# Packed attention and a gated MLP: the first attention re-tiled, its softmax in 32x32 blocks, and its queues in another order

## The chip, the core and the metric

The kernel runs on one core of a Trainium2 chip. The metric is the device time of one execution in microseconds (us). The engines are PE (TensorE, matmuls into PSUM), DVE (VectorE), ACT (ScalarE), POOL (GpSimd) and SP (which here only issues transfers). Each engine works off its own queue in order. An instruction that waits holds up all that stands behind it on its engine.

## The reference

Eight batches of eight heads are attended twice: 32 packed queries p attend to 576 keys and values, and the 576 queries then attend to the 32 results. A gated MLP follows over all 4608 rows.

```python
p_packed = sm_attn(p, k, v)            # per batch and head: 32 x 64
out = sm_attn(q, p_packed, p_packed)   # 576 x 64
x = out.transpose(0, 2, 1, 3).reshape(4608, 512)
h = x @ w_in                           # 512 -> 2048
g = h * clip(h + 3, 0, 6) / 6
return g @ w_out                       # 2048 -> 512
```

w_in and w_out arrive as 64-bit floats; the kernel makes 32-bit ones of them on the chip.

## The kernel before

**Folding.** The product of the second attention with w_in is folded: m = p_packed @ w_in is formed per batch (32 rows per head, two groups g of four heads, so 128 rows per group), and the first product of the MLP is a.T @ m, with a the second softmax. Values are split in two parts (hi, lo) so that three fast matmuls make one exact product: a_hi and a_lo, m_hi and m_lo, g_hi and g_lo (gh, gl), wo_hi and wo_lo.

**Stages.** Batch 0 goes through `first_attention` (line 456), which I call the head: transposes on PE, the packed scores `s1` (line 560), `pack` (line 612), the second scores and softmax `s2` (line 627), and the first product of step 0 by `gemm1` (line 441). `first_moe` (line 894) then runs the sixteen steps f of batch 0 (f is a block of 128 of the 2048 columns); batch 1's attention is woven in from step 4 on. The loop from line 991 does batches 1 to 7, each with the next batch's attention woven in.

**A step of `first_moe`.** PE: first product of step f (`gemm1`, twelve matmuls into the one tile ps_h0), then `u_m0` of step f+1 (line 187, needs w_in of that step), then the second products of step f-1 (`gemm2`, line 904, needs gh, gl, wo_hi, wo_lo). ACT: the Relu of line 951 reads ps_h0. DVE: the gate of line 952 reads it too and so sets it free. ACT writes gh (line 960), POOL subtracts to gl (line 962), and both do the same for the last 64 rows (bnd_hi, bnd_lo).

**Making weights.** `narrowed` (line 125) turns 64-bit words into floats in four steps: two ACT passes (lines 139 and 141), a shift on DVE (line 145), an addition on POOL (line 149). `w_in_step` does it for w_in of a step; `w_out_step` does it for w_out (tile x_out) and then writes wo_hi on ACT (line 159) and wo_lo on DVE (line 161). I write w_in(2), x_out(0), wo_hi(0) for the ones of a step. Each tile of 64-bit words has two buffers, so the load of a step waits for POOL's addition two steps back.

**What sets the order.** In the head and in steps 0 to 3 PE, DVE, ACT and POOL run in the order in which the program is written (`tc.manual_schedule`). Pieces are generators, and `step(part, n)` or `next(part)` runs one to the next `yield`, so the list of such calls (lines 724 to 799) is the order of the queues. From step 4 (IN_ORDER) on a scheduler orders the woven attention. `warm(n)` issues n matmuls of zeros; WARM holds their counts.

## Time and profile before

| | before |
|---|---|
| median of 3 runs | 757.79 us (756.15 to 761.76) |
| profiled execution | 757.65 us, span 755.9 us |
| granted clock of TensorE, mean | 0.995 |
| PE busy | 735.9 us (97%) |
| ACT busy | 387.2 us (51%) |
| DVE busy | 345.5 us (46%) |
| POOL busy | 279.9 us (37%) |
| DMA | 55.98 MB, mean 74 GB/s |

The span is the time from the first to the last instruction of the profiled execution. A busy PE is not PE at its peak, since matmuls are pipelined and their ends are modelled. The chain of work that ended last spends 79% of the span on PE, 6% on DMA and 5% on DVE. The edit lies in the first 40 us and in the first steps of `first_moe`.

### The profile page before, as it was taken

To read this page: it belongs to the slowest core of one execution; us is meant where nothing else is said; L and a number is where in the kernel's file an instruction comes from. 1 tells how busy PE (TensorE), PEld (TensorE's weight loads), DVE (VectorE), ACT (ScalarE), POOL (GpSimd) and SP (SyncE) were. 2 spreads that over 40 slices of the span, in tenths; PEclk is the share of its full clock that TensorE was granted. 3 is DMA by queue.
4 is the path that set the end of the run, shared out by engine and by line. 5 is a ranking of instruction groups with operands and counts; after the bars stand their busy time and mean duration, and the time that the engine had idled before them with its cause. 6 is when DMAs were issued, how large, how long until landed. Compare 5 with 4: busy or idle time off the path is not lost.

```text
span 755.9 us, 13998 instructions
## 1 busy us (share of the span) xinstructions
PE 735.9 (97%) x5197; PEld 581.3 (77%) x5197; DVE 345.5 (46%) x714; ACT 387.2 (51%) x922; POOL 279.9 (37%) x415
## 2 busy tenths in 40 slices
PE   7898999999999999999999999999999999999998
PEld 5775776778777876878777886788787887788886
DVE  3676888432563365342733446342643527321121
ACT  4687874543445445553455535563354635553343
POOL 0487782422233224332333223333232333343332
PEclk9999899999999999999999999999999999999999
DMA  8869964104410541043310523024220210000010
GB/s 260 254 146 215 263 186 83 56 16 93 96 32 31 102 73 45 1 91 69 63 43 1 120 52 78 1 60 96 47 61 1 61 33 29 1 29 0 2 42 29
DMA packets 191205, 55.98 MB, mean 74 GB/s; under 512 B 173216, under 2 KB 184480, under 8 KB 191136
## 3 DMA queue, kind: packets, MB, share of 16 engines
q1 hardware_dynamic: 191136, 55.08, 31.5%
q8 instruction: 41, 0.67, 0.4%
q14 instruction: 28, 0.23, 0.1%
HBM read 45.61 MB, written 9.44 MB: 73 GB/s over the span
## 4 chain that ended last, share of the span: by engine, by line
PE 79%; DMA 6%; DVE 5%; SPq 4%; ACT 3%; issue 2%; POOL 1%; DVEq 0%; POOLq 0%; ACTq 0%
PE acc L853 46%; PE ps_hh L824 23%; PE ps L265 6%; SPq L213 3%; DMA raw_in<-in_moe_w_in_dram 2%; DMA nat<-in_q_dram 2%; PE ps L320 1%; DVE tr L398 1%; DMA nat<-in_k_dram 1%; PE ps_h L448 1%; PE ps L304 1%; DMA v_nat<-in_v_dram 1%; POOL x_out L149 1%; DVE w_in_sb L145 0%; ACT raw_in L139 0%
## 5 line engine op out<-in xcount | busy, mean ns | idle before, releaser
L842 POOL TENSOR_TENSOR g<-t,g 128x256 fp32r<-128x256 f32 x224 | 168.1, 754 | 410.0 <-ACT g L841 384.5
L853 PE MATMUL acc<-wo_hi,g 128*128 128x512 f32 x896 | 316.5, 394 | 1.3 <-ACT g L841 1.3
L837 DVE SCALAR_TENSOR_TENSOR t<-t,ps_hh 128x320 f32<-128x320 f32 (+1 forms) x224 | 100.1, 449 | 252.1 <-ACT t L836 252.0
L836 ACT ACTIVATE t<-ps_hh,three 128x320 f32<-128x320 f32 (+1 forms) x224 | 112.5, 503 | 177.9 <-PE ps_hh L824 167.1
L853 PEld LDWEIGHTS acc<-wo_hi,g 128*128 128x128 f32 x896 | 167.8, 188 | 35.8 <-issue 4.0
L853 PE MATMUL acc<-wo_lo,g 128*128 128x512 f32 x448 | 177.5, 396 | 0.0
L841 ACT CAST g<-t 128x256 fp32r<-128x256 f32 x224 | 90.4, 405 | 94.1 <-DVE t L837 92.8
L824 PE MATMUL ps_hh<-a_hi,m_hi 128*128 128x320 f32 (+1 forms) x448 | 136.1, 304 | 0.5 <-DVE t L837 0.5
L824 PE MATMUL ps_hh<-a_lo,m_hi 128*128 128x320 f32 (+1 forms) x448 | 132.7, 296 | 0.0
L824 PE MATMUL ps_hh<-a_hi,m_lo 128*128 128x320 f32 (+1 forms) x448 | 132.7, 296 | 0.0
L824 PEld LDWEIGHTS ps_hh<-a_hi,m_hi 128*128 128x128 f32 x448 | 84.4, 188 | 34.5 <-issue 19.5
L853 PEld LDWEIGHTS acc<-wo_lo,g 128*128 128x128 f32 x448 | 84.5, 189 | 11.9 <-issue 1.7
L824 PEld LDWEIGHTS ps_hh<-a_lo,m_hi 128*128 128x128 f32 x448 | 84.5, 189 | 8.2 <-issue 0.9
L824 PEld LDWEIGHTS ps_hh<-a_hi,m_lo 128*128 128x128 f32 x448 | 84.5, 189 | 1.7 <-issue 1.3
L398 DVE STREAM_TRANSPOSE tr<-nat 128x576 f32<-128x576 f32 x56 | 41.9, 765 | 30.9 <-PE ps L265 13.3
L388 DVE TENSOR_TENSOR m_lo<-ps,m_hi 128x512 fp32r<-128x512 f32 x56 | 36.1, 683 | 34.8 <-ACT m_hi L387 34.8
L848 POOL TENSOR_TENSOR bnd_lo<-t,bnd_hi 128x64 fp32r<-128x64 f32 x112 | 39.3, 351 | 0.0
L387 ACT CAST m_hi<-ps 128x512 fp32r<-128x512 f32 x56 | 30.1, 589 | 9.8 <-PE ps_hh L824 7.7
L265 PE MATMUL ps<-w_in_sb,pps 64*32 64x512 f32 x448 | 34.3, 601 | 0.5 <-DVE m_lo L388 0.5
L962 POOL TENSOR_TENSOR gl<-t,gh 128x512 fp32r<-128x512 f32 x16 | 23.4, 1464 | 20.6 <-ACT gh L960 11.8
L853 PE MATMUL acc<-wo_hi,gh 128*128 128x512 f32 x64 | 27.0, 421 | 3.5 <-ACT gh L960 3.5
L149 POOL TENSOR_TENSOR w_in_sb<-w_in_sb,raw_in 128x512 int32<-128x512 int32 x14 | 19.5, 1392 | 26.6 <-ACT raw_in L141 17.7
(170 smaller groups left out, 860.2 us busy)
## 6 DMA issues: line engine op xcount, KB each, us to landing
out_dram<-osb SPq DMA_DIRECT2D x36, 256.0 KB, 2.1
nat<-in_k_dram SPq DMA_DIRECT2D x112, 72.0 KB, 2.5
nat<-in_q_dram SPq DMA_DIRECT2D x112, 72.0 KB, 2.6
raw_in<-in_moe_w_in_dram SPq DMA_DIRECT2D x14, 512.0 KB, 5.9
raw_out<-in_moe_w_out_dram SPq DMA_DIRECT2D x14, 512.0 KB, 5.4
v_nat<-in_v_dram SPq DMA_DIRECT2D x56, 128.0 KB, 2.8
spare<-in_k_dram SPq DMA_DIRECT2D x2, 512.0 KB, 4.8
raw<-in_moe_w_in_dram SPq DMA_DIRECT2D x2, 512.0 KB, 4.1
```

The costliest lines, as they stand in the source:

```text
L149: nc.gpsimd.tensor_tensor(out=xi, in0=xi, in1=low, op=ALU.add)
L265: nc.tensor.matmul(banks[x][NPK * a:NPK * a + NPK, :n], rows[half, a], c, start=True, stop=True)
L387: nc.scalar.copy(out=hi[:, x], in_=ps)
L388: nc.vector.tensor_sub(out=lo[:, x], in0=ps, in1=hi[:, x].bitcast(F32))
L398: nc.vector.transpose(out=t, in_=state.pop(("nat", which, b, a)))
L824: nc.tensor.matmul(h[:, :n], mm[:, g, fs], aa[:, t0:t0 + n], start=(g == 0 and i == 0), stop=(g == NG - 1 and i == 2),)
L836: nc.scalar.activation(out=t[:, :n], in_=h, func=AF.Relu, bias=three)
L837: nc.vector.scalar_tensor_tensor(out=t[:, :n], in0=t[:, :n], scalar=6.0, in1=h, op0=ALU.min, op1=ALU.mult)
L841: nc.scalar.copy(out=gh, in_=tm)
L842: nc.gpsimd.tensor_sub(out=gl, in0=tm, in1=gh.bitcast(F32))
L848: nc.gpsimd.tensor_sub(out=bnd_lo[:, slot:slot + REM], in0=tb, in1=bh.bitcast(F32))
L853: nc.tensor.matmul(acc, gg, ww[:, f], start=(f == 0 and i == 0), stop=(f == NF - 1 and i == 2),)
```

## The change

- Keys and queries of batch 0 are transposed two heads to a matmul (`turn_rows`, 4 matmuls of 128 rows), where the queries took 8 matmuls in halves of the array.
- Scores (`products`) and second scores have the packed rows as 32 output partitions per head; the second scores come out as 128 packed rows by 576 queries, not as queries by packed rows. The second softmax `s2` then works as in later batches: DVE transposes blocks of 32x32, takes maximum, difference and sum, and transposes back. PE's transposes of z go away. Group 0 is done in one piece (its multiplication and a_lo on POOL), group 1 in two halves (on DVE).
- `pack` computes 32 output rows per head (20 matmuls of 64 columns, where there were 10 of 128), writes the result twice beside each other, transposes once, and POOL builds the block-diagonal pp_bd and p_bd (`blocks_of`), which DVE and ACT did.
- The scores of heads 0 to 3 run before the keys of heads 4 to 7 are transposed.
- Loads: fewer and larger ones; p and the last 64 keys are issued from ACT; w_in(0) is loaded behind the last queries, not ahead of them.
- Weights: the head ends with w_in(0), w_in(1) made and only the ACT passes of x_out(0) and x_out(1) done. The rest of x_out(0) comes in step 0 ahead of gh; all of w_in(2), the rest of x_out(1) and x_out(2) come behind gh of step 0.
- The copies of t to gh and bnd_hi in a step take both halves of the rows at once, in another row order; the stores of batch 0 follow it.

```diff
-WARM = (3, 2, 2, 1, 3)
+WARM = (3, 2, 3, 3)
...
+        def products(s, g, rows, cols):
+
+            for h in range(4):
+                for x in range(2):
+                    half = slice(64 * x, 64 * x + 64)
                     nc.tensor.matmul(
+                        s[32 * h:32 * h + 32, x, :2 * P],
+                        rows[half, 4 * g + h],
+                        cols[h // 2][half, h % 2],
                         start=True,
                         stop=True,
                     )
...
         def pack(g, et, etr, rinv, vt):
-            ps = pv_ps[:, g, :2 * D]
+
+            ps = pv_ps[:, g, :D]
...
-                for x in range(2):
+                for h in range(4):
                     nc.tensor.matmul(
-                        ps[64 * x:64 * x + 64],
-                        l[:, 64 * x:64 * x + 64],
-                        vt[x][:n, :, c],
+                        ps[NPK * h:NPK * h + NPK],
+                        l[:, NPK * h:NPK * h + NPK],
+                        vt[:n, h, c],
...
+            heads = slice(4 * g, 4 * g + 4)
+            (nc.vector.tensor_copy if g else nc.scalar.copy)(out=pp[:, heads].rearrange("p h n -> p (h n)"), in_=ps)
+            blocks_of(pp, pp_bd, heads)
...
+            for w in parts:
+                for x in range(2 // halves):
+                    o = w.start * NPK + x * HS
+                    nc.vector.transpose(out=flat[:, o:o + HS], in_=s[:, o // HS])
+                yield
+                nc.vector.reduce_max(out=mx[:, w], in_=z[:, w], axis=AX.X)
+                yield
+                nc.vector.tensor_sub(out=z[:, w], in0=z[:, w], in1=across(mx, w))
+                nc.scalar.activation(out=z[:, w], in_=z[:, w], func=AF.Exp, scale=scale)
+                yield
+            for w in parts:
+                nc.vector.reduce_sum(out=den[:, w], in_=z[:, w], axis=AX.X)
+                nc.vector.tensor_scalar_add(den[:, w], den[:, w], 1e-9)
+                nc.vector.reciprocal(den[:, w], den[:, w])
+                (nc.vector if g else nc.gpsimd).tensor_mul(out=z[:, w], in0=z[:, w], in1=across(den, w))
+                yield
+                nc.vector.transpose(out=at[:, cols(w)], in_=flat[:, cols(w)])
+                state["hi"] = nc.scalar.copy(out=hi[:, cols(w)], in_=at[:, cols(w)])
+                yield
...
+        nc.scalar.dma_start(out=p_nat, in_=p[0].rearrange("(g h) i d -> (h i) g d", g=NG))
         k1 = load_k0(1)
...
+        nc.scalar.dma_start(out=kr[:REM], in_=k[0, :, 4 * P:].rearrange("h r d -> r h d"))
...
-        load_w(0, ("in",))
-        q2, q3 = (load_pair(q, 2 + a, spare(3, a)) for a in range(2))
-        load_w(0, ("out",))
+        q2, q3 = (load_q(2 + a, spare(3, a)) for a in range(2))
+        load_w(0)
...
-        return h, {2: win2}, {1: wout1, 2: wout2}
+        return h, {0: wout0, 1: wout1}
...
-                step(m_(f + 1))
-            step(in_(f + 2), 4)
+            step(m_(f + 1))
+            if f:
+                step(in_(f + 2), 4)
...
-            rest(out_(f + 1))
-            step(out_(f + 2), 3 if f else 1)
+                step(out_(f + 2), 3)
...
-            nc.scalar.copy(out=gh, in_=t[:, :4 * P])
-            nc.scalar.copy(out=bnd_hi[:, slot], in_=t[:, 4 * P:])
-            nc.gpsimd.tensor_sub(out=gl, in0=t[:, :4 * P], in1=gh.bitcast(F32))
-            nc.gpsimd.tensor_sub(out=bnd_lo[:, slot], in0=t[:, 4 * P:], in1=bnd_hi[:, slot].bitcast(F32))
-            step(out_(f + 2))
+            for part, hi, lo in ((slice(0, 2 * P), gh, gl), (slice(2 * P, HS), bnd_hi[:, slot], bnd_lo[:, slot])):
+                hi, lo = (x.rearrange("p (a n) -> p a n", a=2) for x in (hi, lo))
+                nc.scalar.copy(out=hi, in_=tv[:, :, part])
+                nc.gpsimd.tensor_sub(out=lo, in0=tv[:, :, part], in1=hi.bitcast(F32))
+            if f:
+                step(out_(f + 2))
+            else:
+                step(in_(2), 4)
+                rest(out_(1))
+                step(out_(2), 4)
```

Three places show how queues are moved. The first is PE at the start of the head, before the change: spare is the tile of the keys, kt their transposes, ktr those of the last 64 keys, pt that of p, ps_w the scores.

```order
L494 MATMUL ps_t<-ident,spare_104 128x128 x8
L519 MATMUL ps_t<-ident,p_nat_106 64x128 x4
L506 MATMUL ps_t<-ident,k_rest_108 128x64 x4
L494 MATMUL ps_t<-ident,spare_104 128x128 x8
L565 MATMUL ps_w<-kt_155,pt_169 32x256 x4
L565 MATMUL ps_w<-kt_162,pt_169 32x256 x4
L573 MATMUL ps_w<-ktr_178,p_bd 64x64 x2
L565 MATMUL ps_w<-kt_185,pt_169 32x256 x4
```

The same place with the change, where rows are the transposed keys and rest those of the last 64.

```order
L490 MATMUL ps_t<-ident,spare_104 128x128 x8
L527 MATMUL ps_t<-ident,p_nat_106 64x128 x4
L504 MATMUL ps_t<-ident,rest_nat_109 128x64 x4
L540 MATMUL ps_w<-rows_149,pt_163 32x256 x4
L540 MATMUL ps_w<-rows_156,pt_163 32x256 x4
L552 MATMUL ps_w<-rest_172,p_bd 64x32 x4
L490 MATMUL ps_t<-ident,spare_104 128x128 x8
L596 MATMUL ps_t<-ident,e_205 128x128 x4
L597 MATMUL ps_t<-ident,e_205 64x128
L540 MATMUL ps_w<-rows_192,pt_163 32x256 x4
```

The scores of heads 0 to 3 moved ahead of the second eight transposes of keys, and the transposes of their exponentials e ahead of the other scores.

The second place is POOL around the end of the head, before the change. raw_out_134 and raw_out_138 hold the words of w_out of steps 0 and 1, raw2 those of step 2 and raw3 those of step 3; the first gl is that of step 0, the second that of step 1, and zr0 belongs to the head's softmax.

```order
L149 TENSOR_TENSOR x_out_326<-x_out_326,raw_out_134 128x512
L649 MEMSET dn0_431 128x4
L677 TENSOR_TENSOR zr0_429<-zr0_429,dn0_431 64x128
L149 TENSOR_TENSOR x_out_490<-x_out_490,raw_out_138 128x512
L149 TENSOR_TENSOR w_in_sb0_321<-w_in_sb0_321,raw2_140 128x512
L962 TENSOR_TENSOR gl_524<-t_516,gh_523 128x512
L963 TENSOR_TENSOR bnd_lo_83<-t_516,bnd_hi_82 128x64
L149 TENSOR_TENSOR x_out_521<-x_out_521,raw2_140 128x512
L149 TENSOR_TENSOR w_in_sb0_321<-w_in_sb0_321,raw3_143 128x512
L962 TENSOR_TENSOR gl_568<-t_556,gh_567 128x512
```

With the change, from the last row of the head's softmax on POOL (a_lo of group 0):

```order
L671 TENSOR_TENSOR a_lo_348<-at_346,a_hi_347 128x576
L149 TENSOR_TENSOR w_in_sb0_375<-w_in_sb0_375,raw_in_130 128x512
L149 TENSOR_TENSOR x_out_488<-x_out_488,raw_out_128 128x512
L944 TENSOR_TENSOR gl_494<-t_483,gh_493 128x512
L944 TENSOR_TENSOR bnd_lo_83<-t_483,bnd_hi_82 128x64
L149 TENSOR_TENSOR w_in_sb0_375<-w_in_sb0_375,raw2_134 128x512
L149 TENSOR_TENSOR x_out_503<-x_out_503,raw_out_132 128x512
L149 TENSOR_TENSOR x_out_510<-x_out_510,raw2_134 128x512
L149 TENSOR_TENSOR w_in_sb0_375<-w_in_sb0_375,raw3_137 128x512
L944 TENSOR_TENSOR gl_551<-t_539,gh_550 128x512
```

Ahead of gl of step 0 there stands x_out(0), and w_in(2) and x_out(1), which stood ahead of it, stand behind it; between the two gl there are four additions, not two.

The third place is ACT from the head's last a_hi to the Relu of step 1, before the change (t is written by the Relu, raw3 holds the words of step 3):

```order
L695 CAST a_hi_467<-ps_t_479 128x320
L951 ACTIVATE t_516<-ps_h0_456,three_78 128x576
L159 CAST wo_hi_80<-x_out_490 128x512
L960 CAST gh_523<-t_516 128x512
L961 CAST bnd_hi_82<-t_516 128x64
L139 ACTIVATE raw3_143<-raw3_143 128x512
L141 ACTIVATE raw3_143<-raw3_143 128x512
L951 ACTIVATE t_556<-ps_h0_534,three_78 128x576
```

With the change, from the Relu of step 0 on (x_out_488 and x_out_503 are those of steps 0 and 1; raw2 and raw3 hold the words of steps 2 and 3):

```order
L932 ACTIVATE t_483<-ps_h0_448,three_78 128x576
L204 CAST m_hi_406<-ps1_478 128x2x128
L159 CAST wo_hi_80<-x_out_488 128x512
L943 CAST gh_493<-t_483 128x512
L943 CAST bnd_hi_82<-t_483 128x64
L139 ACTIVATE raw2_134<-raw2_134 128x512
L141 ACTIVATE raw2_134<-raw2_134 128x512
L159 CAST wo_hi_80<-x_out_503 128x512
L139 ACTIVATE raw2_134<-raw2_134 128x512
L141 ACTIVATE raw2_134<-raw2_134 128x512
L139 ACTIVATE raw3_137<-raw3_137 128x512
L141 ACTIVATE raw3_137<-raw3_137 128x512
```

The row behind these is the Relu of step 1. Between the two Relus there were five instructions, and now there are eleven, among them wo_hi(1) and all four passes of step 2's words.

## Rows read from the trace of the kernel before

**Rows 1.** Table by stage: stretch, length; busy us of each engine; clock, DMA share, GB/s

```profile
42.37:53.47 11.10, 10.81 (x66) 8.43 (x65) 7.86 (x12) 9.53 (x20) 8.80 (x9) 1.00 0.42 117
53.47:70.66 17.19, 16.58 (x102) 11.84 (x100) 11.64 (x19) 12.31 (x27) 14.07 (x13) 1.00 1.11 235
...
75.48:81.38 5.90, 5.90 (x28) 3.90 (x28) 4.49 (x13) 4.71 (x12) 3.92 (x4) 0.71 1.10 315
...
300.00:755.00 455.00, 451.15 (x3073) 364.35 (x3072) 173.38 (x375) 217.16 (x543) 152.86 (x258) 1.00 0.19 42
```

**Rows 2.** Timeline of PE: start us, us, engine, line, operation, out<-in, count [idle before <-releaser]

```profile
8.95 0.66 PE L565 MATMUL ps_w<-kt,pt 64*32 64x256 f32 x16
...
20.77 0.43 PE L616 MATMUL ps_w<-spare,etr 64*64 64x128 f32 x4
...
35.25 0.29 PE L448 MATMUL ps_h<-a_hi,m_lo 128*128 128x288 f32 x1
...
37.16 0.40 PE L448 MATMUL ps_h<-a_hi,m_hi 128*128 128x288 f32 x1 [0.32 <-DVE t L952]
...
38.95 0.66 PE L193 MATMUL ps<-w_in_sb,pp_bd 128*64 128x128 f32 x8
...
42.37 0.29 PE L448 MATMUL ps_h<-a_hi,m_hi 128*128 128x288 f32 x1
...
45.59 0.50 PE L853 MATMUL acc<-wo_hi,gl 128*128 128x512 f32 x1 [0.21 <-POOL gl L962]
...
75.48 0.51 PE L853 MATMUL acc<-wo_hi,gh 128*128 128x512 f32 x1 [2.98 <-ACT gh L960]
```

**Rows 3.** Timeline of ACT: the head's first weights, and the hand-over to step 0

```profile
16.99 0.66 ACT L139 ACTIVATE raw_in<-raw_in 128x512 f32<-128x512 f32 x1 [2.60 <-DMA raw_in<-in_moe_w_in_dram]
...
35.58 0.74 ACT L951 ACTIVATE t<-ps_h,three 128x576 f32<-128x576 f32 x1 [1.55 <-PE ps_h L448]
36.99 0.62 ACT L159 CAST wo_hi<-x_out 128x512 fp32r<-128x512 f32 x1 [0.68 <-POOL x_out L149]
37.52 0.61 ACT L960 CAST gh<-t 128x512 fp32r<-128x512 f32 x1
...
38.19 0.69 ACT L139 ACTIVATE raw<-raw 128x512 f32<-128x512 f32 x1
```

**Rows 4.** Timeline of DVE: pt in the head, and step 0

```profile
6.85 0.42 DVE L523 COPY pt<-ps_t 128x256 f32<-128x256 f32 x1
...
36.35 0.75 DVE L952 SCALAR_TENSOR_TENSOR t<-t,ps_h 128x576 f32<-128x576 f32 x1 [0.53 <-ACT t L951]
37.65 1.13 DVE L161 TENSOR_TENSOR wo_lo<-x_out,wo_hi 128x512 fp32r<-128x512 f32 x1 [0.54 <-ACT wo_hi L159]
38.70 1.51 DVE L145 TENSOR_SCALAR x_out<-raw 128x512 int32<-128x512 int32 x1
```

**Rows 5.** Timeline of POOL around the hand-over

```profile
35.56 1.40 POOL L149 TENSOR_TENSOR x_out<-x_out,raw_out 128x512 int32<-128x512 int32 x1 [3.05 <-DVE x_out L145]
36.92 1.31 POOL L149 TENSOR_TENSOR w_in_sb<-w_in_sb,raw 128x512 int32<-128x512 int32 x1
38.21 1.71 POOL L962 TENSOR_TENSOR gl<-t,gh 128x512 fp32r<-128x512 f32 x1
39.88 0.51 POOL L963 TENSOR_TENSOR bnd_lo<-t,bnd_hi 128x64 fp32r<-128x64 f32 x1
40.35 1.49 POOL L149 TENSOR_TENSOR x_out<-x_out,raw 128x512 int32<-128x512 int32 x1
```

**Rows 6.** Chain that ended last, a later batch's pack: start us, us, what

```profile
88.52 1.36 PE ps L320 x40
```

**Rows 7.** Single lines of later batches' softmax: ns min/median/max, first and last start, form

```profile
L356 DVE STREAM_TRANSPOSE z<-ps x28: 432/441/484, 109.4 to 626.5; 128x288 f32<-128x288 f32 x28
...
L364 DVE TENSOR_REDUCE mx<-z x14: 733/743/753, 118.4 to 627.6; 128x18 f32<-128x576 f32 x14
```

**Rows 8.** Timeline of SP's issues: step 6's w_out

```profile
52.78 0.35 SPq L122 DMA_DIRECT2D raw_out<-in_moe_w_out_dram  x1
```

More of the change, by code (lines that the diff above doesn't have):

```diff
@@ L510, in turn_k_rest, with blocks_of @@
                 )
-            t = gp.tile([P, NPAIR, REM], F32, name="ktr0", tag="osb", bufs=2)
-            nc.vector.tensor_copy(out=t.rearrange("p a r -> p (a r)"), in_=ps)
-            return t
+            yield
+            t = gp.tile([P, NPAIR, REM], F32, name="rest0", tag="osb", bufs=2)
+            copy(out=t.rearrange("p a r -> p (a r)"), in_=ps)
+            yield t
+        def blocks_of(rows, blocks, heads):
+            for h in range(2):
+                half = slice(64 * h, 64 * h + 64)
+                nc.gpsimd.tensor_copy(
+                    out=blocks[half, heads.start // 2:heads.stop // 2, NPK * h:NPK * h + NPK],
+                    in_=rows[half, heads].rearrange("p (a x) n -> p a x n", x=2)[:, :, h],
+                )
         def turn_p(nat):
@@ L697, in s2, with across, cols @@
-            for cs, ps in turned_z:
-                state["lo"] = nc.vector.tensor_sub(out=lo[:, cs], in0=ps, in1=hi[:, cs].bitcast(F32))
+            n = T // halves
+            parts = [slice(i, i + n) for i in range(0, T, n)]
+            def across(t, w):
+                return t[:, w].unsqueeze(2).to_broadcast([P, n, NPK])
+            def cols(w):
+                return slice(w.start * NPK, w.stop * NPK)
+            for w in parts:
[4 more added lines that the diff above has]
+                nc.vector.reduce_max(out=mx[:, w], in_=z[:, w], axis=AX.X)
+                yield
+                nc.vector.tensor_sub(out=z[:, w], in0=z[:, w], in1=across(mx, w))
+                nc.scalar.activation(out=z[:, w], in_=z[:, w], func=AF.Exp, scale=scale)
+                yield
@@ L699, in s2 @@
+            for w in parts:
+                state["lo"] = (nc.vector if g else nc.gpsimd).tensor_sub(
+                    out=lo[:, cols(w)], in0=at[:, cols(w)], in1=hi[:, cols(w)].bitcast(F32)
+                )
             state["a", 0, g] = (hi, lo)
@@ L734, in first_attention @@
-        tq = [turned(nat, act) for nat in (q0, q1, q2, q3)]
-        step(a0)
-        step(a1)
+        tkr = turn_rest(kr, act)
+        step(tkr)
+        ktr = next(tkr)
+        a0, a1 = s1(0), s1(1)
+        step(a0, 2)
+        tk = [turn_rows(k1, act), turn_rows(k1[:, 2:], dve, gp, "g", 4)]
+        step(tk[0])
+        kt.append(next(tk[0]))
+        step(tk[1])
+        step(a0)
+        kt.append(next(tk[1]))
+        e0 = next(a0)
+        et0 = turn_e(e0, act, dve)
+        r0 = next(a0)
@@ L737, in first_attention @@
+        step(a1, 3)
+        tq = [turn_rows(nat, copy) for nat, copy in ((q0, act), (q1, dve), (q2, act), (q3, dve))]
         step(tq[0])
-        e0 = next(a0)
         qt = [next(tq[0])]
+        pv_ps = wide()
+        pp = gp.tile([P, H, NPK], F32, name="pp0", tag="osb", bufs=2)
+        pack0 = pack(0, *et0, r0, v0)
+        step(pack0, 2)
         e1 = next(a1)
-        r0 = next(a0)
-        et0 = turn_e(e0, dve, dve)
-        r1 = next(a1)
-        step(tq[1])
-        qt.append(next(tq[1]))
@@ new lines, in first_attention @@
+        r1 = next(a1)
+        b0, b1 = s2(0, 1), s2(1, 2)
+        m0 = u_m0(0, tail)
+        win0, wout0, win1, wout1 = w_in_step(0), w_out_step(0), w_in_step(1), w_out_step(1)
+        step(b0)
+        tqr = turn_rest(qr, act)
+        step(tqr)
+        qtr = next(tqr)
+        pack1 = pack(1, *et1, r1, v1)
+        step(b0)
+        step(pack1)
+        step(win0, 2)
+        step(b0)
+        step(pack1)
+        step(b0)
+        step(tq[2])
+        step(pack1)
+        step(tq[3])
+        qt.append(next(tq[2]))
@@ L777, in first_attention @@
+        step(b0)
+        rest(pack1)
+        qt.append(next(tq[3]))
+        rest(win0)
+        step(b1, 2)
+        step(b0)
+        step(wout0, 2)
+        warm(WARM[3])
         step(m0, 2)
         step(b1, 3)
+        step(b0)
+        rest(b0)
         rest(m0)
-        rest(b0)
-        step(m1, 2)
-        step(wout0)
-        win2, wout2 = w_in_step(2), w_out_step(2)
-        step(win2, 2)
-        step(wout2, 2)
+        step(b1, 3)
+        step(win1, 2)
+        step(b1)
+        step(wout1, 2)
@@ L786, in first_attention @@
+        rest(win1)
+        step(b1, 3)
         warm(WARM[1])
@@ L892, in moe, with first_moe @@
                 second(2)
-    def first_moe(h, w_in, w_out):
+    def first_moe(h, w_out):
         ahead = attention(1) if B > 1 else iter(())
-        accs, m0 = [], {}
+        accs, w_in, m0 = [], {}, {}
         def attend(f, n):
```

247 lines of the change are left out of this document (69 added, 178 removed).

## Prediction

> **What bounds the kernel now.** I read the table by stage first [rows 1]. From 300 to 755 us TensorE is busy 451 of 455 us: what is lost ahead of that stays lost, and nothing there is edited. So the question is when the first product loop (line 931, sixteen steps f) runs. Between 42.37 and 53.47 us all engines are close: ACT 9.53, POOL 8.80 and PE 10.81 of 11.10 us, at a DMA share of 0.42. From 53.47 on DMA is full (share 1.11).
>
> The timelines then show the hand-over from the first attention (the head) to the loop. The head's last matmul starts at 35.25 us, so the first product of step 0 is complete at 35.54; I call this time T. Step 1's first product starts at 37.16, step 2's at 42.37 [rows 2]. On ACT, T is followed by the Relu (35.58), wo_hi and gh [rows 3]; on DVE by the gate (36.35) [rows 4]. POOL in the same stretch adds up x_out of step 1 and w_in of step 2 (35.56, 36.92), before gl of step 0 at 38.21 [rows 5]. The reader is to see that POOL's two weight additions cost nothing here: they lie beside Relu, gate and gh.
>
> **The change, part by part.**
>
> *Head, first half.* Scores of heads 0 to 3 no longer wait for the transposes of heads 4 to 7. They need pt, copied from 6.85 for 0.42 us [rows 4], so they start at 7.3 instead of 8.95 [rows 2]. They also need p_bd, now two POOL copies of 64x128 that no row shows: below 0.1 there is nothing on POOL, and a 128x64 subtraction takes 0.51 [rows 5]; I take 0.3 each, nearer the second (ends for the range: 0.2 and 1.0 for both). The pack in 32-column parts doubles the matmuls: the later batches run this very form, 40 records in 1.36 us [rows 6]; of the present form the second pack's last 4 records end at 21.20 [rows 2]. I take 1.36. By the new queues: scores 0 at 7.3, exponentials at 9.6, transposes of e at 10.4, scores 1 at 11.1, pack 0 from 12.6 to 13.9, second scores 0 at 15.4, pack 1 from 17.3 to 18.6: 2.6 us ahead of 21.20. The transfers are the same bytes in fewer issues; p and the last keys go by ACT's queue, which idles until its first copy, so I cost that at nothing (without that cover: the two issues, about 1 us). w_in of step 0 is now behind q2 and q3. It was the one transfer ACT waited for (2.60 us, to 16.99) [rows 3]; 512 KB more ahead of it make it 0 to 1.9 us later. I take 0.7, to 17.7. Behind it in ACT's queue stand the copy of q2 and the exponentials of second scores 0, wanted at 20.5: 0.9 us of cover.
>
> *Head, second half.* Now DVE sets the pace. From pn of pack 1 on it has 30 operations: four on 128x576 at 0.72 each (a maximum there took 0.743 [rows 7], less the overlap of neighbours), fourteen on halves (a 128x288 transpose took 0.441 [rows 7]; 0.42), and two copies, two weight shifts, m_lo, pn and six small ones, which I put at 3.7 in all (the first six at 0.28 to 0.61, the small ones at 0.24). Sum 2.9 + 5.9 + 3.7 = 12.5 us, from 18.7 to 31.2, plus 0.3 waiting for POOL's multiplication and 0.4 for the last matmuls. So T = 31.9 instead of 35.54: the head is 3.6 us shorter (bounds from the POOL copies, w_in and DVE's pitch: 2.4 to 4.8).
>
> *Step 0.* The head used to convert weights on the way. Now wo_hi(0), all of w_in(2) and x_out(2), and x_out(0) and x_out(1) from DVE's shift on come behind T. The three POOL additions x_out(0), w_in(2), x_out(1) go from beside the head onto the path, as the order of POOL and ACT shows. Replayed with T = 31.9:
> - Relu 0.65, gate 0.70, m_lo 0.35 and DVE's shift 0.45 lead to 34.05 (DVE's queue is in order: the shift for x_out(0) stands behind the gate). POOL's x_out(0) takes 1.3 (1.40 and 1.31 in [rows 5]): 35.35.
> - wo_hi 0.53 and gh 0.51 [rows 3] follow in order: 36.45. gl took 1.71 with DVE beside it; 1.4 here: 37.9. bnd_lo 0.5: 38.4. w_in(2) 1.3: 39.7. x_out(1) 1.3: 41.0.
> - PE finishes step 1's first product at 35.1 and then has u_m0 of step 2, which needs w_in(2), ahead of all second products of step 0. It starts at 39.7 instead of 38.95 [rows 2]. The 3.6 us are gone, and PE is 0.75 behind.
> - ACT's queue holds wo_hi(1) (41.6), both passes of w_out(2) (0.69 each alone, 1.15 for two [rows 3]; 42.75) and of w_in(3) (43.9) ahead of step 1's Relu, though that product has been complete since 35.1. Relu and gate end at 45.25, and step 2's first product starts at 45.3 instead of 42.37: 2.9 late.
> - x_out(2) is complete at 44.05, where it began at 40.35 and took 1.49 [rows 5]: 2.2 late. gh(1) ends at 47.05, gl(1) at 48.35, so the first matmul that waits for gl starts at 48.4 instead of 45.59 [rows 2]: 2.8 late.
>
> DVE's wo_lo (1.13) and shift (1.51) [rows 4] run long where POOL is busy; this adds up to 0.5, already in the 1.4 for gl.
>
> *After that.* Behind these rows all five queues hold the same order in both kernels, so a lag is carried. It shrinks only where a step has slack: a replay of steps 2 to 4 gives back some 0.4 us in all. The DMA burst does not take it up: it is released by POOL's x_out(4), upon which SP issues at 52.78 [rows 8], 2.4 late now. The profiled execution took 757.65 us (span 755.9 and 1.75 around it; median of the runs 757.79, so 0.14 lies between them). Forecast: 757.65 - 3.6 + 6.1 = 760.2, where 6.1 is the 2.5 us of lag plus the 3.6 consumed. Its own range is 758.7 to 762.
>
> **The rivals.**
>
> *The clock falls (763.6).* After a wait of 2.98 us PE resumed at 75.48 [rows 2], and the granted clock of 75.48 to 81.38 was 0.71 [rows 1]: with two levels, 1 (2.4 GHz) and 0.5 (1.2 GHz), 58% of 5.90 us at the lower, so 1.7 us of PE work lost. The new kernel has PE waiting from 35.1 to 39.7, 4.6 us, and PE is sparse from 20 to 31 too (about 3 of each 5 us). A fall at 39.7 delays the second products of step 0 by 1.7, but they are followed by a wait to 45.3 in any case, so most is covered; falls in the head lengthen T, and one that outlasts 45 is paid in full. Two falls paid in full: 760.2 + 3.4 = 763.6. Against it: the head's matmuls are few, and the wait covers much. The Trainium skill (TensorE: Matmul & The Clock Gate, What's actually happening) says that the clock's default state is the throttled one and that activity releases it. By that rule a fall in the 4.6 us wait is certain, and the time is between 760.2 and 763.6. The trace agrees at 75.48.
>
> *The loop gives the lag back (754.0; the other side).* POOL is busy 8.80 of 11.10 us between 42.37 and 53.47: a fifth of each step is slack. If the late additions fill that slack instead of queueing behind gh and wo_hi, the lag shrinks by 0.21 x 11.1 = 2.3 us by step 4, and the 3.6 of the head come through from there on as far as the burst allows: 757.65 - 3.6 = 754.0. It decides where the lag at step 5 is below zero. For it: PE, ACT and POOL all have slack. Against: POOL waits for ACT and ACT for POOL in turn, in order, so the slack sits between dependent instructions.
>
> *The change does not reach the end (757.5).* DMA is full from 53.47 to 70.66; if the burst's end is set by bytes rather than by its release, neither gain nor lag passes it. For it: share 1.11. Against: share 0.42 just before, so the burst starts when it is released.
>
> **How the numbers follow.** Chances: forecast 0.50, clock 0.13, loop gives back 0.22, no change at the end 0.15. The range 756.5 to 764.0 takes in the forecast, the clock and no change (0.78), and with them the bounds of the POOL copies and of w_in. One per cent is 7.6 us, about what a measurement of this kernel (756.15 to 761.76) can tell from no change: below 750.2 lies only a head much shorter than I can make it (0.03), above 765.2 the clock with a lag of over 4 us (0.06), the rest is within (0.91).
>
> **What would show it.** Right, if the first product of step 0 is complete at 31 to 33 us; if PE then waits some 4 us ahead of u_m0 of step 2, released by POOL's w_in addition; if step 1's Relu runs on ACT at about 44; and if the second products of steps 2 to 4 are 2 to 3 us later than before. Wrong in the head, if T is outside 31 to 33; wrong in the loop, if T is right and the first product of step 5 is not later than before; wrong in the clock, if the granted clock is below 0.9 between 20 and 50 us.

## The result, and the profile after

The changed kernel takes 763.7 us (median of 10 runs, of which nine lie between 762.6 and 766.54 and one took 2453.7) against 757.82. The ratio, without that one run, is 1.0081, with a 95% interval of 1.0061 to 1.0102. That is 6.1 us slower. The forecast was 760.2, only 2.5 us slower. The sign was right, and the time lies inside the range of 756.5 to 764.0, though close under its upper end and outside the forecast's own 758.7 to 762. The profiled execution took 762.9 us (span 761.1).

The table by stage of the changed kernel (stretch, length; busy us of PE, PEld, DVE, ACT, POOL; clock, DMA share, GB/s):

```profile
25.00:30.00 5.00, 2.82 (x20) 1.99 (x17) 4.83 (x10) 2.22 (x5) 2.13 (x2) 1.00 1.06 277
30.00:35.00 5.00, 4.70 (x20) 2.94 (x18) 4.23 (x11) 2.70 (x6) 1.30 (x1) 0.66 0.70 108
35.00:40.00 5.00, 3.29 (x14) 2.90 (x12) 1.99 (x4) 2.22 (x6) 1.30 (x2) 0.68 0.86 205
40.00:45.00 5.00, 1.87 (x12) 1.36 (x12) 1.48 (x3) 1.75 (x5) 4.39 (x4) 0.84 0.40 135
45.00:50.00 5.00, 4.46 (x19) 3.45 (x18) 4.16 (x7) 5.00 (x11) 2.61 (x2) 0.79 0.30 107
...
53.47:70.66 17.19, 17.00 (x109) 12.83 (x107) 12.28 (x19) 14.17 (x29) 14.31 (x13) 1.00 0.78 177
...
300.00:755.00 455.00, 454.19 (x3094) 367.72 (x3093) 175.50 (x379) 219.06 (x549) 154.33 (x262) 1.00 0.19 41
```

From 300 us on nothing is lost, as before [rows 1]. From 40 to 45 us PE is busy 1.87 of 5 us, while POOL is busy 4.39: PE waits for POOL. The full DMA burst, which stood at 1.11 between 53.47 and 70.66, is now at 0.78 there, because it starts later.

PE's timeline from the head's end (start us, us, line, operation, count [idle before <-releaser]):

```profile
34.85 0.29 PE L436 MATMUL ps_h<-a_hi,m_lo 128*128 128x288 f32 x1
36.85 0.58 PE L436 MATMUL ps_h<-a_hi,m_hi 128*128 128x288 f32 x1 [1.71 <-DVE t L933]
...
43.20 0.73 PE L193 MATMUL ps<-w_in_sb,pp_bd 128*64 128x128 f32 x8 [3.13 <-POOL w_in_sb L149]
43.86 0.80 PE L833 MATMUL acc<-wo_hi,gh 128*128 128x512 f32 x1
...
48.90 0.37 PE L436 MATMUL ps_h<-a_hi,m_hi 128*128 128x288 f32 x1 [0.54 <-DVE t L933]
...
54.22 0.29 PE L436 MATMUL ps_h<-a_hi,m_hi 128*128 128x288 f32 x1
```

Against [rows 2]: T is 35.14 (before 35.54), u_m0(2) starts at 43.20 (38.95), step 2's first product at 48.90 (42.37, so 6.5 later). Step 3's comes at 54.22 and was at 47.99 before: 6.2 later. Of that lag 5.2 us are left at the end of the span.

POOL's timeline behind the head:

```profile
37.45 1.30 POOL L149 TENSOR_TENSOR x_out<-x_out,raw_out 128x512 int32<-128x512 int32 x1 [5.14 <-DVE x_out L145]
40.00 1.27 POOL L944 TENSOR_TENSOR gl<-t,gh 128x512 fp32r<-128x512 f32 x1 [1.25 <-ACT gh L943]
41.23 0.50 POOL L944 TENSOR_TENSOR bnd_lo<-t,bnd_hi 128x64 fp32r<-128x64 f32 x1
41.69 1.45 POOL L149 TENSOR_TENSOR w_in_sb<-w_in_sb,raw 128x512 int32<-128x512 int32 x1
43.11 1.28 POOL L149 TENSOR_TENSOR x_out<-x_out,raw_out 128x512 int32<-128x512 int32 x1
```

ACT's timeline from the Relu of step 0 to that of step 1:

```profile
35.18 0.74 ACT L932 ACTIVATE t<-ps_h,three 128x576 f32<-128x576 f32 x1 [1.11 <-PE ps_h L436]
...
38.78 0.62 ACT L159 CAST wo_hi<-x_out 128x512 fp32r<-128x512 f32 x1 [2.60 <-POOL x_out L149]
...
44.42 0.62 ACT L159 CAST wo_hi<-x_out 128x512 fp32r<-128x512 f32 x1 [3.25 <-POOL x_out L149]
...
47.23 0.73 ACT L932 ACTIVATE t<-ps_h,three 128x576 f32<-128x576 f32 x1
```

ACT and POOL wait for each other in turn, and step 1's Relu, whose product was complete since 40, stands behind the eleven instructions.

DVE's timeline in the head's second half:

```profile
19.63 0.35 DVE L618 TENSOR_SCALAR pn<-ps_w,rinv 128x128 f32<-128x128 f32 x1
...
23.26 0.87 DVE L663 TENSOR_SCALAR den<-den 128x18 f32<-128x18 f32 x1
...
25.29 0.76 DVE L658 TENSOR_TENSOR z<-z,mx 128x288 f32<-128x288 f32 x1
...
27.95 1.28 DVE L658 TENSOR_TENSOR z<-z,mx 128x288 f32<-128x288 f32 x1
...
29.63 0.17 DVE L663 TENSOR_SCALAR den<-den 128x9 f32<-128x9 f32 x1
...
31.19 0.41 DVE L662 TENSOR_REDUCE den<-z 128x9 f32<-128x288 f32 x1
31.64 0.70 DVE L663 TENSOR_SCALAR den<-den 128x9 f32<-128x9 f32 x1
...
34.10 0.46 DVE L671 TENSOR_TENSOR a_lo<-at,a_hi 128x288 fp32r<-128x288 f32 x1 [0.16 <-ACT a_hi L668]
```

POOL's timeline of the same stretch:

```profile
22.80 1.28 POOL L149 TENSOR_TENSOR w_in_sb<-w_in_sb,raw_in 128x512 int32<-128x512 int32 x1 [0.60 <-DVE w_in_sb L145]
24.57 1.16 POOL L665 TENSOR_TENSOR z<-z,den 128x576 f32<-128x576 f32 x1 [0.48 <-DVE den L664]
27.51 1.40 POOL L671 TENSOR_TENSOR a_lo<-at,a_hi 128x576 fp32r<-128x576 f32 x1 [1.78 <-ACT a_hi L668]
31.02 1.30 POOL L149 TENSOR_TENSOR w_in_sb<-w_in_sb,raw_in 128x512 int32<-128x512 int32 x1 [2.10 <-ACT raw_in L141]
```

The addition of 1e-9 takes 0.17 alone and 0.70 beside POOL, and 0.87 beside POOL on the 128x18 of group 0 (0.18 on 128x20 in the kernel before). Four operations are long in this way, and each ends 0.0 to 0.3 us behind the POOL operation beside it (24.13 and 24.08, 26.05 and 25.73, 29.23 and 28.91, 32.34 and 32.32). A sum in such a stretch (31.19) is not longer.

### The profile page after: what moved, and what is told of

Its sections match the earlier page's. It is cut to its first block, busy times and chain, and to the rows that moved or that the text cites. A ratio compares the mean times of both kernels' runs of the same rounds, so it can differ in the third digit from the quotient of the medians.

```text
span 761.1 us, 13961 instructions
## 1 busy us (share of the span) xinstructions
PE 736.1 (97%) x5183; PEld 579.3 (76%) x5183; DVE 349.1 (46%) x713; ACT 386.9 (51%) x918; POOL 282.2 (37%) x417
## 4 chain that ended last, share of the span: by engine, by line
PE 81%; DVE 6%; DMA 4%; ACT 3%; issue 2%; POOL 2%; SPq 1%; DVEq 0%; POOLq 0%; ACTq 0%
PE acc L833 47%; PE ps_hh L804 23%; PE ps L265 6%; DMA nat<-in_k_dram 2%; PE ps L320 1%; DVE tr L386 1%; PE ps_h L436 1%; SPq L213 1%; PE ps L304 1%; DMA raw_out<-in_moe_w_out_dram 1%; DMA nat<-in_q_dram 1%; POOL w_in_sb L149 1%; POOL x_out L149 1%; DMA spare<-in_k_dram 1%; DVE mx L352 1%
## 5 line engine op out<-in xcount | busy, mean ns | idle before, releaser
L436 PE MATMUL ps_h<-a_hi,m_hi 128*128 128x288 f32 x64 | 21.3, 333 | 6.0 <-DVE t L933 4.8
```

The lines of the kernel that those rows point to most:

```text
L436: nc.tensor.matmul(h[:, hf, :HS], mm[:, g, fs], aa[:, hf * HS:(hf + 1) * HS], start=(g == 0 and i == 0), stop=(g == NG - 1 and i == 2),)
```

## The experiments

All but e10 start from the changed kernel. "Step 2" is the start of step 2's first product on PE, "start" the time that the first eight transposes took. These rows are of one profiled execution each. The ratios are of all runs, to the kernel before, with their 95% intervals. Where the intervals of two kernels overlap, I take the difference between them as not resolved. Pack 1 is the pack of heads 4 to 7.

| | start | T | step 1's Relu | step 2 | step 2 - T | ratio |
|---|---|---|---|---|---|---|
| before | 1.06 | 35.54 | 39.34 | 42.37 | 6.83 | 1 |
| changed | 1.94 | 35.14 | 47.23 | 48.90 | 13.76 | 1.0081 (1.0061 to 1.0102) |
| e1, more zeros at the start | 1.07 | 35.15 | 47.24 | 49.40 | 14.25 | 1.0047 (1.0025 to 1.0068) |
| e2, w_in(2) early | 1.94 | 34.97 | 45.60 | 47.26 | 12.29 | 1.0064 (1.0041 to 1.0087) |
| e3, x_out(0) early | 1.94 | 38.75 | 48.33 | 49.98 | 11.23 | 1.0058 (1.0037 to 1.0079) |
| e4, no 1e-9 | 1.06 | 33.71 | 45.80 | 47.46 | 13.75 | 1.0065 (1.0042 to 1.0088) |
| e5, loads by SP | 1.94 | 34.66 | 46.79 | 48.44 | 13.78 | 1.0081 (1.0057 to 1.0106) |
| e6, six conversions early, no 1e-9 | 1.94 | 34.52 | 40.16 | 43.39 | 8.87 | 1.0004 (0.9985 to 1.0022) |
| e7, e1 and e5 and e6 | 1.71 | 33.83 | 39.79 | 43.74 | 9.91 | 0.9976 (0.9961 to 0.9991) |
| e8, zeros in the waits | 1.94 | 37.76 | 49.84 | 51.49 | 13.73 | 1.0092 (1.0071 to 1.0114) |
| e9, e7 with wo_lo(0) later and zeros | 1.04 | 33.57 | 38.86 | 40.55 | 6.98 | 0.9968 (0.9952 to 0.9984) |
| e10, before with late conversions | 1.94 | 35.10 | 46.92 | 48.60 | 13.50 | 1.0060 (1.0039 to 1.0080) |
| e11, group 0 on DVE | 1.06 | 36.00 | 48.07 | 49.73 | 13.73 | 1.0104 (1.0074 to 1.0133) |

**The start of the head: e1 and e5.**

```diff
-WARM = (3, 2, 3, 3)
+WARM = (5, 2, 3, 3)
```

> The changed kernel with five instead of three matmuls on zeros ahead of the first keys. In the changed kernel the first eight transposes took 1.94 us from 5.32 (1.06 in the kernel before) though the granted clock reads 1.00, and the first scores started at 8.95 instead of the forecast 7.3. Theory A (TensorE had been idle for 1.16 us, against 0.97 before, and runs slowly for it): with the wait filled the eight transposes take about 1.1 us, the first scores start at 7.4 to 7.6, pack 1 ends near 18.5 instead of 19.57, T comes 1.0 earlier (34.1) and the time is 762.7 instead of 763.7. Rival (the loads that now go by ACT's queue, or something else at the start, slow it): the rows stay at 1.9 us and 8.95, and the time at 763.7.

PE's timeline of e1 at the start:

```profile
5.36 1.07 PE L490 MATMUL ps_t<-ident,spare 128*128 128x128 f32 x8
6.36 0.66 PE L527 MATMUL ps_t<-ident,p_nat 128*64 128x128 f32 x8
8.81 0.43 PE L504 MATMUL ps_t<-ident,rest_nat 64*128 64x64 f32 x4 [1.79 <-DMA rest_nat<-in_k_dram]
9.17 0.66 PE L540 MATMUL ps_w<-rows,pt 64*32 64x256 f32 x16
```

TensorE ran at full speed, and the scores still started at 9.17: theory A falls. The last rows of the keys, now loaded by ACT's queue, had not landed. The ratio is 0.3% under the changed kernel's, but the intervals overlap, and no row from T on is earlier. That the zeros make the fast start is not shown either: e4 and e11 start fast with three, e7 slowly with five.

```diff
-        nc.scalar.dma_start(out=p_nat, ...)
+        nc.sync.dma_start(out=p_nat, ...)
-        k1 = load_k0(1)
-        nc.scalar.dma_start(out=kr[:REM], ...)
+        nc.sync.dma_start(out=kr[:REM], ...)
+        k1 = load_k0(1)
```

> The changed kernel with p and the last rows of the keys loaded again by SP's queue, behind the first keys and ahead of the second (the order of the kernel before); nothing else moves. In the changed kernel the last rows (rest_nat, 128 KB) took 6.9 us to land by ACT's queue (4.3 by SP's in the kernel before), and where TensorE ran at full speed from the start, in the two runs with more matmuls on zeros or without the additions of 1e-9, their transposes waited for that load, 1.79 and 1.42 us, until 8.81 and 8.42. Theory A (that landing sets the start of the first scores): the transposes of the last rows follow those of p at once, the first scores start at 7.4 to 7.6 (8.6 if TensorE starts slowly) instead of 8.95, pack 1 ends 1.0 to 1.3 earlier than 19.57, T comes at about 34.0 instead of 35.14, and the time is 762.6 instead of 763.7. Rival (the second keys, now behind two more loads, or ACT's chain behind them, are what sets pack 1): the first scores start earlier, but pack 1 ends at 19.3 or later, and the time stays within 0.4 of 763.7.

This run started slowly, and the scores began at 8.62, as forecast for that case; pack 1 ended at 19.09 (19.57), and T came 0.48 earlier, where 1.1 was forecast. The time did not resolve it. Among the profiles with a fast start pack 1 ended at 19.59, 19.19 and 19.16 with the loads on ACT's queue (e1, e4, e11) and at 18.17 with them on SP's (e9). By that one profile, which has other edits too, the load costs 1.0 to 1.4 us where TensorE starts fast. It costs 0.3 to 0.5 where TensorE starts slowly (19.40, 19.42 and 19.57 in e2, e6 and the changed kernel, 19.09 and 19.07 in e5 and e7).

**DVE beside POOL: e4 and e11.**

```diff
-                nc.vector.tensor_scalar_add(den[:, w], den[:, w], 1e-9)
```

> The changed kernel without the three additions of 1e-9 to the second softmax's sums (each sum is at least 1, where 1e-9 is less than half a unit of float32). They took 0.87, 0.17 and 0.70 us on DVE, two of them beside a POOL addition, and the fourth such stretch was a subtraction of 1.28 us for 0.45. Theory A (on DVE some operations stand still until POOL's operation beside them ends, so that DVE's list takes 14.9 us instead of the forecast 12.5, and the waits belong to these operations' kind): all 1.74 us go from DVE's list, T comes at 33.5 to 33.7 instead of 35.14, and the time is 762.1. Rival B (the wait moves to the reciprocal or the next operation): only 0.5 to 0.7 us go, T at 34.5, the time 763.1. Rival C (the head's end is not set by DVE but by POOL and ACT): T stays at 35.1 and the time at 763.7.

T came 1.43 earlier: 0.37 from the head's start, 1.07 from DVE's list (19.26 to 33.12, 13.86 us, where it was 14.93). Of the 1.74 us taken away 0.67 came back: the next operations of the same kind then stood beside POOL (a subtraction went from 0.76 to 1.14, a multiplication from 0.46 to 0.80). The truth lies between A and B. The span fell by 1.3 us with T; the ratio is 1.2 us under the changed kernel's, which isn't resolved.

```diff
-                (nc.vector if g else nc.gpsimd).tensor_mul(...)
+                nc.vector.tensor_mul(...)
...
-                state["lo"] = (nc.vector if g else nc.gpsimd).tensor_sub(
+                state["lo"] = nc.vector.tensor_sub(
```

> The changed kernel with the second softmax's multiplication and a_lo of heads 0 to 3 on DVE instead of POOL. Theory A (DVE's operations that read two tiles in SBUF, or copy from SBUF to SBUF, stand still until POOL's operation beside them ends): the two subtractions of 128x288 that took 0.76 and 1.28 us in the changed kernel take 0.45, since POOL has nothing beside them; the additions of 1e-9 beside POOL's weight additions stay at 0.87 and 0.70. DVE's list gains two operations of about 0.72 and loses 1.14, so T comes 0.3 later, up to 0.8 with a wait for a_hi, and the time is 764.0 to 764.5: moving 2.56 us of work from POOL to DVE costs next to nothing. Rival (these operations are long for another reason): they stay at 0.76 and 1.28, T comes 1.4 later, and the time is 765.1 or more.

DVE's timeline of e11 in the head's second half:

```profile
22.86 0.87 DVE L663 TENSOR_SCALAR den<-den 128x18 f32<-128x18 f32 x1
...
25.73 0.46 DVE L658 TENSOR_TENSOR z<-z,mx 128x288 f32<-128x288 f32 x1
...
27.62 0.76 DVE L671 TENSOR_TENSOR a_lo<-at,a_hi 128x576 fp32r<-128x576 f32 x1 [0.74 <-ACT a_hi L668]
...
29.62 0.46 DVE L658 TENSOR_TENSOR z<-z,mx 128x288 f32<-128x288 f32 x1
...
32.48 0.70 DVE L663 TENSOR_SCALAR den<-den 128x9 f32<-128x9 f32 x1
```

With POOL idle beside them both subtractions take 0.46 instead of 0.76 and 1.28, and the additions of 1e-9 beside POOL's weight additions stay at 0.87 and 0.70. The mechanism is shown. My price was too low: DVE's list grew by 1.24 us (to 16.17), with 0.74 of it a wait for a_hi, and from pack 1's end to T it took 1.27 us more, where I gave 0.3 to 0.8. That the time grew by more too isn't resolved (1.0104 against 1.0081, the intervals overlap).

**The queues behind T: e2, e3, e10.** e2 has a win2 = w_in_step(2) in the head:

```diff
-        step(b1, 3)
+        step(b1, 2)
+        step(win2, 2)
+        step(b1)
...
         rest(b1)
+        rest(win2)
```

> The changed kernel with the conversion of w_in of step 2 moved ahead: its two passes on ACT go between the last two a_hi casts (ACT is idle there from 32.26 to 33.63), its shift and POOL's addition right behind the head's last a_lo. Theory A (POOL's and ACT's queues behind T hold the loop): w_in(2) is complete at about 36.4 instead of 43.14, the wait of 3.13 us ahead of u_m0(2) is gone (it starts at 40.1), step 1's Relu has two passes less ahead of it (45.9 instead of 47.23), step 2's first product starts at 47.5 instead of 48.90, and the time is 762.3 instead of 763.7. Rival B (the granted clock, 0.66 to 0.84 from 30 to 50 us, costs the time): the shorter wait lets the clock rise earlier, u_m0(2) and the second products of step 0 come 3 us earlier, and the time falls by up to 3 us, to 760.7. Rival C (only the start of the head matters): no change, 763.7.

The wait ahead of u_m0(2) was gone (39.83), and step 2 came at T + 12.29, 1.47 sooner after T; 1.4 was forecast. The ratio is 1.3 us under the changed kernel's, but the intervals overlap.

```diff
         rest(m0)
+        step(wout0)
         step(b1, 3)
         step(win1, 2)
+        step(wout0)
```

> The changed kernel with DVE's shift and POOL's addition of x_out(0) put back into the head (POOL is idle from 28.91 to 31.02); nothing else moves. Theory A (the additions on POOL behind T are the path): T comes 0.4 to 0.8 us later (35.5 to 35.9: one shift of 0.42 more on DVE, and what DVE loses beside POOL), but gh(0) no longer waits for x_out(0) to be added (37.3 instead of 39.31), gl(0) follows 2.0 earlier, then w_in(2) and x_out(1), and step 1's Relu comes at about 45.2 instead of 47.23. Step 2's first product starts at 46.9 instead of 48.90; the time is 761.7. Rival B (the clock): what is lost to the lower clock stays, so 763.7 plus the 0.4 to 0.8 of T: 764.3.

Step 2 came at T + 11.23, 2.53 sooner. T itself was 3.6 late: in this profile TensorE stayed slow until 16.5 us, so that pack 1 ended 2.57 later, and DVE's list took 0.61 more. Behind step 2 the clock took part of the gain back: the granted clock fell to 0.50 (51 to 52 us), and step 3 came at 56.72, only 1.1 sooner after T than in the changed kernel, though step 2's gate had ended at 54.16. By the ratios the runs are 1.7 us under the changed kernel's, near the forecast 2.0, but the intervals overlap.

e10 is the other side, edited in the kernel before (the loop's part as in the changed kernel's diff):

```diff
-        step(wout0, 3)
+        step(wout0, 2)
...
-        step(wout0)
-        win2, wout2 = w_in_step(2), w_out_step(2)
-        step(win2, 2)
-        step(wout2, 2)
...
-        rest(wout0)
-        step(wout1, 2)
         gemm1(h, 0, 1)
```

> The kernel before, with its own head, its loads and its first softmax, but with the conversions placed as in the changed kernel: x_out(0) and x_out(1) from DVE's shift on, and all of w_in(2) and x_out(2), behind the head's last product, in the changed kernel's order of step 0. Theory A (this placing alone is the loop's loss): T comes 0.5 to 1.5 earlier than 35.54, since DVE and POOL have less to do in the head; step 1's Relu comes at T + 12, step 2's first product at T + 13.8, that is 47.8 to 48.8 instead of 42.37, and the time is 763.2 to 764.2 against 757.8. Rival (the loss needs the new head: its softmax on DVE, or the clock that falls in it): 758 to 760. The run also shows whether TensorE's slow first 2 to 11 us, which six of eight profiles of the changed kernel and its variants have, come with the loads of the kernel before, too.

PE's timeline of e10:

```profile
42.90 1.12 PE L193 MATMUL ps<-w_in_sb,pp_bd 128*64 128x128 f32 x8 [4.28 <-POOL w_in_sb L149]
...
48.60 0.34 PE L448 MATMUL ps_h<-a_hi,m_hi 128*128 128x288 f32 x1
```

The old head with the late conversions shows the same wait and nearly the same step 2 (T + 13.50 for 13.76), and is 4.5 us slower by the ratio (1.0060; 5.4 to 6.4 was forecast). The placing alone makes the loop's loss; the new head is not needed for it.

**The clock: e8, e6, e7, e9.** e8:

```diff
         gemm1(h, 0, 1)
+        warm(3)
...
                     gemm1(h, f, g)
+            if f == 1:
+                ps = ps_o.tile([P, 512], F32, name="ps_t", tag="acc")
+                for _ in range(3):
+                    nc.tensor.matmul(ps[:, :2 * P], zeros[:, :P], zeros, start=True, stop=True)
             step(m_(f + 1))
```

> The changed kernel with three matmuls on zeros behind the head's last matmul (where TensorE waited 1.71 us) and three behind step 1's first product (where it waited 3.13 us for w_in(2)); nothing else moves. Theory A (the lower clock is covered, since step 2's first product waits for step 1's gate at 48.00 in any case): u_m0(2) starts at 43.2, step 2's first product at 48.9, and the time is 763.7 (within 0.5). Rival (the clock, which the waits let fall, costs the time): the granted clock from 35 to 50 us rises to 1.00, the second products of step 0 take 2.9 instead of 4.5 us, step 2 starts earlier, and the time falls by 1.5 to 3 us.

The row of e8's table by stage in which the second products of step 0 lie (46.42 to 49.48):

```profile
45.00:50.00 5.00, 3.64 (x20) 2.59 (x20) 1.61 (x3) 2.94 (x6) 3.05 (x3) 1.00 0.31 109
```

The granted clock was 1.00, and these products took 3.1 us instead of 4.5; step 2 still came at T + 13.73. In the changed kernel's profile the slow clock in the loop is covered. It isn't always: in e1 the clock was 0.50 from 45 to 49 us, and step 2 came at 49.40, though step 1's gate had ended at 48.76. That is why its T + 14.25 is 0.5 more than the changed kernel's.

e6 leaves out the additions of 1e-9 as e4 does, places x_out(0)'s shift and addition in the head as e3 does, then:

```diff
+        step(win2, 2)
         step(b1)
+        step(wout0)
...
         rest(b1)
+        rest(win2)
+        step(wout1, 2)
+        rest(wout0)
```

> The changed kernel without the additions of 1e-9 to the second softmax's sums (as in the run before, where T came 1.4 earlier), and with six conversions placed ahead again: x_out(0)'s shift and addition in the head, its wo_hi behind the last a_hi, the two passes of w_in(2) on ACT between the last a_hi casts, and behind the last a_lo DVE's shifts of w_in(2) and x_out(1), POOL's additions of both, and wo_lo(0). Theory A (the three POOL additions and the ACT passes behind T make T + 13.8 out of T + 6.8 for step 2's first product): T at 34.1 to 34.5, step 1's Relu at T + 5.2 instead of T + 12.1, step 2's first product at T + 6.9, that is 41.0 to 41.4 instead of 48.90 (42.37 in the kernel before), and the time is 756.1 to 756.6. Rival B (the clock of 0.66 to 0.84 from 30 to 50 us is what costs): PE still runs at the lower level and comes to step 2 at 43 or later; 758 to 759. Rival C (the loop's lag behind step 2 has another source): 760 or more.

The Relu came at T + 5.6, and the 6.1 us were gone (ratio 1.0004). Of the 5.5 us by which step 2 came sooner, 0.6 are T's and 4.9 the loop's. But step 2 was 2.0 later after T than forecast, and the time is rival B's, not theory A's. DVE's timeline of e6 around step 0's gate, and the row of its table by stage:

```profile
34.19 1.78 DVE L161 TENSOR_TENSOR wo_lo<-x_out,wo_hi 128x512 fp32r<-128x512 f32 x1
35.90 0.74 DVE L941 SCALAR_TENSOR_TENSOR t<-t,ps_h 128x576 f32<-128x576 f32 x1
```

```profile
35.00:40.00 5.00, 3.22 (x14) 2.97 (x16) 3.94 (x6) 3.89 (x9) 4.24 (x5) 0.50 0.89 231
```

wo_lo(0) stood still beside POOL and held the gate; and from 35 to 40 the clock was at the lower of its two levels (1.2 GHz), so that step 1's first product took 3.15 us (36.78 to 39.93) where it took 1.79 in the kernel before. With the queues out of the way PE is the path, and rival B is right for those 1.4 us; the gate's delay is the other 0.6.

> All pieces together: the conversions ahead and no additions of 1e-9 as in the run above, p and the last rows of the keys by SP's queue, five matmuls on zeros at the start. By theory A it is the run above less the 1.0 to 1.3 us of the head's start: T at 33.0 to 33.4, step 2's first product at 39.9 to 40.3, the time 755.0 to 755.4, some 2.5 us under the kernel before. Rival (the burst of transfers behind step 4 or the clock takes back what the head gains): 757 to 758.

e7 is 0.24% faster than the kernel before. That is 0.6 to 1.0 us short of the forecast, which lies within its interval. In its profile T was 33.83 (33.0 to 33.4 was forecast) and step 2 came only at 43.74, 3.4 to 3.8 later than forecast: wo_lo(0) held the gate again (1.77 us), and PE ran at the lower level here too (0.50 from 35 to 40 us), which is the rival's reason. The span is still 0.2 us under that of the kernel before, whose step 2 was 1.4 earlier; what gave the difference back further on was not followed.

```diff
-WARM = (5, 2, 3, 3)
+WARM = (5, 4, 5, 5)
...
         step(wout1, 2)
-        rest(wout0)
         gemm1(h, 0, 1)
+        warm(4)
```

> The run with all pieces joined, with two more edits. There wo_lo(0) stood on DVE ahead of step 0's gate and took 1.8 us for 0.69 beside POOL's addition, so that the gate ended 0.5 late; it now stands behind the gate. And TensorE, whose granted clock was 0.50 from 35 to 40 us, took 3.15 us for step 1's first product (1.79 in the kernel before), which now lies on the path; six more matmuls on zeros fill its waits from 25 to 34 us, and four stand behind the head's last matmul. Theory A (with the conversions ahead, TensorE itself is the path from step 0's gate on, and the clock counts): step 1's first product starts at T + 1.7 and takes 1.8 us, step 2's first product comes at 41.3 to 41.9 instead of 43.74 (42.37 in the kernel before), and the time is 754.0 to 754.6 against 756.4. Rival (the clock falls in spite of the extra matmuls, or they lengthen the head): step 2 at 43 or later, 756 or more.

PE's timeline of e9 from the head's end, and the row of its table by stage:

```profile
33.28 0.29 PE L436 MATMUL ps_h<-a_hi,m_lo 128*128 128x288 f32 x1
...
35.28 0.37 PE L436 MATMUL ps_h<-a_hi,m_hi 128*128 128x288 f32 x1
...
37.05 0.66 PE L193 MATMUL ps<-w_in_sb,pp_bd 128*64 128x128 f32 x8
...
40.55 0.37 PE L436 MATMUL ps_h<-a_hi,m_hi 128*128 128x288 f32 x1
```

```profile
35.00:40.00 5.00, 5.00 (x32) 4.01 (x31) 4.34 (x7) 4.54 (x9) 4.49 (x4) 1.00 0.98 275
```

The clock stays at 1.00, step 1's first product takes 1.77, and step 2 comes at 40.55, 1.8 earlier than in the kernel before. The ratio is 0.9968: about 2.4 us faster than the kernel before (3.2 to 3.8 was forecast), and part of that comes from leaving out the additions of 1e-9, which the kernel before has. The span of its profile is 2.0 us under e7's (753.7 for 755.7), but the ratios' intervals overlap, so that the gain over e7 isn't resolved.

## Why the prediction was right on the sign and wrong on the size

**Step 0, right.** PE's wait ahead of u_m0(2), released by POOL's w_in addition, the eleven instructions ahead of step 1's Relu, the second products behind them: all are there. The wait was 3.13 us where I had 4.6, because step 1's first product ran at the lower clock level (a granted clock of 0.50 from 36.85 to 40.10; 3.2 us for 1.85); in e1 and e4, where it took 1.8, the wait was 4.53 and 4.54. From T to step 2's first product I had 45.3 - 31.9 = 13.4, measured 13.76; from T to the first matmul that waits for gl 16.5, measured 16.68 (51.82). e2, e3, e6 and e10 show that it is the placing of the conversions.

**Head, the term that was mis-sized.** I gave the head 3.6 us; it gave 0.4. T was 35.14 for 31.9. That is outside the bounds of 2.4 to 4.8, and by my own sign I was wrong in the head. These 3.2 us and the 0.4 of step 0 are the 3.6 by which step 2 came later than forecast (6.5 us for 2.9). Of the 3.2 us:
- 0.9 come from the first half: pn of pack 1 started at 19.63 for 18.7. A step that failed is "p and the last keys go by ACT's queue, which idles until its first copy, so I cost that at nothing". I had priced the issue and not the landing: the 128 KB landed 6.9 us after issue, for 4.3 by SP's queue, and PE's queue has their transposes ahead of the first scores. But in this profile TensorE's slow start, which no forecast had, lies beside that load: PE came to these transposes only at 8.29 and did not wait for it. Without the slow start alone pack 1 ends 0.0 to 0.4 sooner (e1, e4, e11), without the late load alone 0.5 (e5), without both 1.4 (e9). So the load is shown to cost 0.3 to 0.5 of the 0.9 here, and the rest goes only with the two together. POOL's two copies (0.63, assumed 0.6), the pack (0.9, assumed 1.36) and w_in(0) (ACT's pass at 18.05 without a wait) were right or better. In e9, with the loads on SP and a fast start, pack 1 ends at 18.17, for the forecast 18.6. One reading was wrong and cost nothing: w_in(0) was not the one transfer that ACT waited for before, since w_out(0) held it for 1.18 us, to 20.03; in the changed kernel it waits for neither.
- 2.1 come from DVE's list: 14.93 us for the 12.5 plus 0.3. The step that failed is "Sum 2.9 + 5.9 + 3.7 = 12.5". The four stretched operations add 2.35 us; the rest of the list was 0.2 under the sum. I had written that wo_lo and the shift run long where POOL is busy [rows 4], and did not apply it to the head, where four POOL operations of 1.2 to 1.4 us stand beside DVE's list. The Trainium skill (SBUF — State Buffer, SBUF: two separate sides) has the rule: DVE and POOL share a pair of ports, which one of them holds for a whole instruction, so that an operation of DVE with two SBUF inputs, or in a two-port mode, blocks against POOL's. The rows and e11 agree with it.
- 0.2 is the head's last matmuls (0.58 for 0.4).

**After that, right.** The lag was carried: 6.5 at step 2, 6.2 at steps 3 and 4, 5.2 at the end of the span, where I gave back 0.4 (what gave back the last 1.0 was not followed). SP's issue of step 6's w_out moved from 52.78 [rows 8] to 58.95. So "the change does not reach the end" and "the loop gives the lag back" were wrong, the latter because POOL and ACT wait for each other in turn: wo_hi(1) and wo_hi(3) wait 3.25 and 0.97 us for POOL (44.42, 53.53), gl(1) and gl(2) 1.10 and 1.11 us for ACT (50.47, 55.88).

**The clock rival.** By my own sign I was wrong on the clock: it was 0.66 to 0.84 from 30 to 50 us. It fell at about 30 us, after PE had been busy 2.82 of the 5 us before, and so ahead of the wait that I had in view; and it cost nothing in the loop of the changed kernel's profile (e8), though 0.5 us in e1's and 1.4 behind step 2 in e3's. It cost 1.4 us as soon as the queues were mended (e6 against e9). So that the time, 763.7, comes out at this rival's 763.6 is chance, and it is by luck that it lies in the range: the rival's end of the range covered a head that was mis-sized. The Trainium skill's rule (TensorE: Matmul & The Clock Gate, What's actually happening), that the lower level is the default, agrees; what it costs depends on who is the path.
